# Maxima in pairs and a shared PSUM bank: a reordered attention step in a two-layer Fourier and attention kernel

## Chip, core and metric

The kernel runs on one core of one Trainium2 chip. Its time is device microseconds from the first to the last instruction of one execution; three runs are given, and beside them one execution was recorded by the hardware profiler. The engines that matter are PE (matmul), DVE (VectorE), ACT (ScalarE) and POOL (GpSimd). PE writes only to PSUM, which has eight banks of 512 fp32 values for each of 128 partitions; DVE and ACT read them from there.

## What is computed

The input is one sequence of 2048 tokens with 512 features. Two layers are run, and each adds two results to `x`: a Fourier mixing of the normalized `x`, and an attention with 32 heads of 16 values whose keys and values are shared by all heads.

```python
def _A_ref(x, dft_seq_re, dft_seq_im, dft_hid_re, dft_hid_im):
    a = jnp.einsum("bsd,ed->bse", x, dft_hid_re)
    b = jnp.einsum("bsd,ed->bse", x, dft_hid_im)
    return jnp.einsum("ts,bse->bte", dft_seq_re, a) - jnp.einsum("ts,bse->bte", dft_seq_im, b)

def _B_ref(x, wq, wk, wv, wo):
    ...
    scores = jnp.einsum("bhqd,bkd->bhqk", q, k) * (Dh ** -0.5)
    p = _softmax(scores, axis=-1)
    o = jnp.einsum("bhqk,bkd->bhqd", p, v)
    return o.transpose(0, 2, 1, 3).reshape(B, S, H * Dh) @ wo

x = x + _A_ref(_layernorm(x), ...)
x = x + _B_ref(_layernorm(x), wq, wk, wv, wo)
# the same two lines once more
```

All is fp32. The softmax subtracts each row's maximum, so the maximum of every row of 2048 scores must be known before the exponentials of that row.

## The kernel before

The order of the instructions is written out by hand: every engine runs its instructions in the order in which the Python code issues them, and waits for the others by semaphores. Each product of the mixing, of the projections and of the output is made of three reduced-precision products with the high and low parts of its operands (`mm3`, L86 to L89).

**Stages.** A layer has a mixing stage (`phase_a`) and an attention stage (`phase_b`). The mixing stage has 128 iterations `n`, each with four groups of three products into four accumulators (tile "x", two pairs of banks). After every 32 of them come four `y_tile`s, each a sum of 24 products into one bank, and then, among the next iterations, the transposes (`tr_tile`), the key and value projection (`kv`) and the query projection (`q_mm`) of these 512 tokens, each sum in one bank. Score maxima whose keys and queries are ready are found already here (`max_early`, listed in `EARLY` with the iterations over which they are spread: 16 entries of 32 units, 13 of them for later query tiles and kept in "mxe").

**A unit of maximum** is one product of 128 queries (all rows of one head of a pair) with 512 keys into a bank, and one DVE `reduce_max` of that bank to one column. A layer has 1520 such units left for the attention stage: the list `units`, in the order of query tile, head pair, key block, group.

**The attention stage** takes 16 query tiles `i` of 128 queries in 32 steps `s_` each, n = 32 i + s_. One step has:
- `pv`, the value product of the step two before: four products, side by side on the array, into the accumulator "z" (L712). After 16 steps ACT copies it to SBUF (L715).
- four scores (`score`, j = 0 to 3, L698): each 64 rows deep, so that the two groups g = 0 and 1 of heads use the two halves of the array's rows. Two scores share an "x" tile of two banks, and one exponential on ACT reads both banks (L701).
- maxima: `more_max` issues one unit (`max_half`, product at L347, reduction at L348), as many as `owed` allows, three a step. A unit is 64 rows deep as well and stands between the scores: score of group 1-g, one unit, score of group g, two units at most, score, score, one unit at most.
- tasks of the output: at step 12 of the next tile the output projection (`o_proj`): twelve products into a "y" bank, and after each half of them two more units; then the residual sum on DVE (L777). In layer 0 DVE also takes the statistics of the next normalization (steps 14 and 16).
- when a tile's maxima are all there, `max_neg` takes the last maximum on DVE and, two steps later, `max_rows` transposes it on PE into a "y" bank (L376) and ACT copies it out (L378); this happens at step 29 for the next tile, and at step 13 for the second half of tile 0.

**PSUM.** The eight banks are two "x" pairs (four banks), three "y" banks and one "z" bank. "y" serves single maxima, the sums of `y_tile`, `kv`, `q_mm` and the output projection, and the transpose of the maxima; "z" the transposes of the activations and the value accumulator. A tile's first product waits until all reads of the tile that had its bank before are done.

Of the kernel before, what the change touches and what calls it, by code (L numbers as in the profile page):

```python
# [8 lines left out]
F32 = mybir.dt.float32  # L9
F32R = mybir.dt.float32r  # L10
I32 = mybir.dt.int32
AF = mybir.ActivationFunctionType
# [5 lines left out]
P = 128  # L18
# [29 lines left out]
def fnet_mqa_kernel(ctx: ExitStack, tc: tile.TileContext, x_in, ct, dt_, wq, wkv, wo, out):  # L48
# [13 lines left out]
        return sb.tile([P, D], dtype, name=f"row{k}")  # L62

    def bank(tag):
        return ps.tile([P, 512], F32, name=tag, bufs={"y": 3, "z": 1}[tag])

    def pair():
        return ps.tile([P, 2, 512], F32, name="x", bufs=2)

    def split_ps(ps_, hi, lo, neg=False):  # L70
        nc.scalar.activation(hi, ps_, AF.Copy, scale=-1.0 if neg else 1.0)
# [115 lines left out]
    def make_layer(L, src, mid, dst, last):  # L187
# [66 lines left out]
                split_ps(v[0], xth, xtl)  # L254

        def kv(t0, n, xth, xtl, vt=None):
            pk = bank("y")[:, :n * P]
            for k in range(NK):
                mm3(pk, wkvh[:, k, :], wkvl[:, k, :], xth[:, k, :n * P], xtl[:, k, :n * P], k == 0, k == NK - 1)
            cs = slice(t0 * P, (t0 + n) * P)  # L260
            if vt is None:
                vt = half(7)[:64, :n * P]
            nc.scalar.copy(vt[32:64], pk[32:64])
            for g in range(2):
                gs = slice(64 * g, 64 * g + 64)
                nc.scalar.activation(kz[g][gs, cs], pk[gs], AF.Identity, scale=kmask[gs], bias=kone[gs])
            for g in range(2):
                gs = slice(64 * g + 32, 64 * g + 48)
                nc.vector.tensor_sub(kz[g][gs, cs], pk[gs], f(kz[g][gs, cs]))
            return vt  # L270
# [6 lines left out]

        def q_mm(tb, g, xth, xtl):
            wh, wl = st["wqh", g]
            pq = bank("y")  # L280
            for k in range(NK):
                ks = slice(k * P, (k + 1) * P)
                mm3(pq, wh[:, ks], wl[:, ks], xth[:, k, :], xtl[:, k, :], k == 0, k == NK - 1)
            hi = half(4 + 2 * (g % 2), F32R)
            lo = half(5 + 2 * (g % 2), F32R)
            split_act(pq, hi, lo, half(g))
            st["qs", tb, g] = hi, lo
# [41 lines left out]
                        nc.gpsimd.tensor_copy(o.mxp[i][:, :, :, kb], st["mxe"][:, e])  # L329
            return o.mxp[i]  # L330

        def max_one(i, pr, g, c0, n, to):
            pm = bank("y")[:, :n]
            nc.tensor.matmul(pm, o.qT[i][:, pr, :], kz[g][:, c0:c0 + n], start=True, stop=True)  # L334
            nc.vector.reduce_max(to, pm, axis=AX.X)  # L335

        def max_early(e, pr, g):
            i, kb = EARLY[e][:2]
            if "mxe" not in st:
                st["mxe"] = sb.tile([P, len(KEPT), NPAIR, 2], F32, name="mxe")  # L340
            to = st["mxe"][:, KEPT.index(EARLY[e]), pr, g:g + 1] if i else partial(0)[:, pr, g, kb:kb + 1]
            max_one(i, pr, g, kb * 512, 512, to)

        def max_half(i, pr, g, kb):
            pm = bank("y")
            gs = slice(64 * g, 64 * g + KR)
            nc.tensor.matmul(pm, o.qT[i][gs, pr, :], kz[g][gs, kb * 512:kb * 512 + 512], start=True, stop=True)  # L347
            nc.vector.reduce_max(partial(i)[:, pr, g, kb:kb + 1], pm, axis=AX.X)  # L348

        def qT_load(i, k=None):  # L350
            k_ = QSLOT[i] if k is None else k
# [19 lines left out]
            st["ms"] = ms  # L371

        def max_rows(i, p0=0, n=NPAIR, queue=None):
            queue = queue or nc.sync
            pt = bank("y")[:4 * n, :P]
            nc.tensor.transpose(pt, st["ms"].rearrange("p a b c -> p (a b c)"), ident)  # L376
            mt = sb.tile([64, P], F32R, name="mt")[:4 * n, :]
            nc.scalar.copy(mt, pt)  # L378
            for g in range(2):
                for r in range(2):  # L380
                    row = 64 * g + M0 + r
                    q = queue if r else nc.sync
                    q.dma_start(f(o.qT[i][row:row + 1, p0:p0 + n, :]), f(mt[n * (2 * g + r):n * (2 * g + r + 1), :]))

        def y_tile(tb, tt, zh, zl, x1, between={}):
            t = 4 * tb + tt
            y = bank("y")
            tsl = slice(tt * P, (tt + 1) * P)
            for cc in range(2):
                for k in range(NK):  # L390
                    mm3(y, zh[cc][:, k, tsl], zl[cc][:, k, tsl], dh[cc][:, k, :], dl[cc][:, k, :],
                        cc == 0 and k == 0, cc == 1 and k == NK - 1)
                    for fn in between.get(4 * cc + k, ()):
                        fn()
            nc.vector.tensor_add(x1, y, x1)
            nc.gpsimd.dma_start(mid[t], x1)
            ln_stats(x1, t)
# [103 lines left out]
        def phase_a(extra):  # L501
# [20 lines left out]
            for e, (i, kb, k, n0, n1, n2) in enumerate(EARLY):  # L522
                if n0 is not None:
                    add(n0, lambda i=i, k=k: qT_load(i, k))
                for u in range(2 * NPAIR):
                    at = divmod(int(4 * (n1 + u * (n2 - n1) / (2 * NPAIR))), 4)
                    b, n = divmod(at[0], 40)
                    at = (32 * b + n, at[1]) if n < 32 else ("y", b, 4 * (n - 32) + at[1])
                    inner.setdefault(at, []).append(lambda e=e, u=u: max_early(e, u // 2, u % 2))
            zh, zl, x1, vt = {}, {}, {}, {}  # L530
            z = None

# [121 lines left out]
                if g == 0:  # L654
                    v_tr(12, 4, vt[0])
            max_neg(0, 0, HALF, 5)
            for k in range(12):
                more_max()
                if k == 2:
                    max_rows(0, 0, HALF, nc.scalar)  # L660

        early = {e[:2] for e in EARLY}
        units = [(0, pr, g, 3) for pr in range(HALF, NPAIR) for g in range(2)]
        units += [(i, pr, g, kb) for i in range(1, NT) for pr in range(NPAIR) for kb in range(4) for g in range(2)
                  if (i, kb) not in early]
        o.done = o.extra = 0

        def more_max():
            if o.done < len(units) and units[o.done][0] in o.loaded | {0}:
                max_half(*units[o.done])  # L670
                o.done += 1

        def owed(n):
            return min(3 * (n + 1) + 12 + o.extra, len(units)) - o.done

        def done_with(i, pr):
            return all(u[:2] > (i, pr) for u in units[o.done:])

        ptiles = {}

        def score(i, s_, j):
# [4 lines left out]
                k = i * NSTEP + s_  # L686
                ptiles[i, s_] = slot((6, 7, 2)[k % 3]).rearrange("p (j n) -> p j n", j=4)
            w = j // 2
            if i == NT - 1 and jj == 1 and o.done == len(units):
                e = bank("y")  # L690
                nc.tensor.matmul(e, kz[g][64 * g:64 * g + KR, c * P:(c + 1) * P],
                                 o.qT[i][64 * g:64 * g + KR, cp:cp + 4, :], start=True, stop=True)
                nc.scalar.activation(ptiles[i, s_][:, j, :], e, AF.Exp, scale=DH ** -0.5)
                return
            first = "e" not in st
            if first:
                st["e"] = pair()
            nc.tensor.matmul(st["e"][:, g, :], kz[g][64 * g:64 * g + KR, c * P:(c + 1) * P],  # L698
                             o.qT[i][64 * g:64 * g + KR, cp:cp + 4, :], start=True, stop=True)
            if not first:  # L700
# [4 lines left out]
        def pv(i, s_):  # L705
# [6 lines left out]
                nc.tensor.matmul(a[32 * j:32 * j + 32, :], v1[:, c, :], pt[:, j, :], start=c == 0, stop=c == NT - 1)  # L712
            if c == NT - 1:
                oa = half(hf)
                nc.scalar.copy(oa, a)  # L715
                acc[i, hf] = oa

        bt = {}
# [48 lines left out]
        def o_proj(i):  # L767
            for k in range(NK):
                o_mm(k)
                if k % 2 and i < NT - 1:  # L770
                    for _ in range(2):
                        more_max()
                        o.extra += 1
            o_add(i)

        def o_add(i):
# [3 lines left out]
        def finish():  # L780
            i = NT - 1
            oa = acc.pop((i, 1))
            x_load(i)
            pt = bank("y")
            for b in range(4):
                nc.tensor.transpose(pt[:, b * P:(b + 1) * P], oa[:, b * P:(b + 1) * P], ident)
            o_mm(0)
# [5 lines left out]
            for jj in range(2):  # L793
# [1 line left out]
                    on[:, jj * P:(jj + 1) * P].rearrange("p (b g d) -> p b g d", b=4, g=2),  # L795
                    p4[:, :, 2 * jj:2 * jj + 2, :DH],
                    rc[:, :, 2 * jj:2 * jj + 2].unsqueeze(3).to_broadcast([P, 4, 2, DH]), op=ALU.mult)
            pt = bank("y")[:, :256]
            for jj in range(2):
                nc.tensor.transpose(pt[:, jj * P:(jj + 1) * P], on[:, jj * P:(jj + 1) * P], ident)  # L800
            split_ps(pt, bt["oh"][:, 256:], bt["ol"][:, 256:])
# [31 lines left out]
        def phase_b(nxt):  # L833
# [10 lines left out]
            for n in range(NT * NSTEP):  # L844
# [1 line left out]
                if len(behind) == 2:  # L846
                    pv(*behind.pop(0))
                behind.append((i, s_))
                g = units[o.done][2] if o.done < len(units) else 1
                for j, m in ((1 - g, 1), (g, 2), (3 - g, 0), (2 + g, 1)):  # L850
                    score(i, s_, j)
                    for _ in range(m):
                        if owed(n) >= 1:
                            more_max()
                if i == 0 and 2 <= s_ <= 8 and s_ % 2 == 0:
                    q_half_store(14, s_ // 2 - 1)
                if n == 12:
# [21 lines left out]
                nxt.a_start()  # L879
            for at in behind:  # L880
                pv(*at)
            return out_tasks(NT - 1)

        def half_tasks(i):
            return {
# [4 lines left out]
        def out_tasks(i):  # L890
            return {
                1: [lambda: o_store(i, 1), lambda: o_sum(i, 1), lambda: x_load(i)], 5: [lambda: o_inv(i, 1)],
                6: [lambda: o_load(i, 1)], 9: [lambda: o_scale(i, 1)], 10: [lambda: o_hi(i, 1)],
                12: [lambda: o_proj(i)], 14: [lambda: o_stats(i)], 16: [lambda: o_rstd(i)],
                25: [lambda: o_ln(i)], 26: [lambda: o_xnh(i)], 27: [lambda: o_xnl(i)],
            }

# [49 lines left out]
```

## Time and profile before

| | us |
|---|---|
| median of three runs (3771.49 to 3774.22) | 3773.21 |
| profiled execution, first to last instruction | 3768.5 |
| reductions of the attention stage's maxima (L348), DVE busy, 3040 of 684 ns | 1908.7 |
| exponentials of score pairs (L701), ACT busy, 1990 of 1027 ns | 1942.9 |
| value products (L712), PE busy, 8192 records | 1096.2 |
| scores into "x" (L698), PE busy, 2956 records in the largest group | 900.4 |
| maximum products of the attention stage (L347), PE busy, 2272 records in the largest group | 747.8 |
| early maxima (L335 into mxe), DVE busy, 832 | 525.2 |

The lines of the profile that carry the argument stand in the prediction. Busy times are the union of an instruction group's spans. A matmul's span is longer than what it keeps from the next one, since products overlap in the array; distances between starts tell more than durations. "Idle before" is the time in which an engine waited, with the line that ended the wait.

### The profile page before, as it was taken

What the parts mean: (1) busy time and instruction counts of PE and PEld (TensorE: products, weight loads), DVE (VectorE), ACT (ScalarE), POOL (GpSimd) and SP (SyncE); (2) the same over time, 40 slices, a digit from 0 to 9 for tenths busy, and PEclk for the clock granted to TensorE, in tenths of its full rate; (3) what the DMA queues carried; (4) which work ended last, traced back from release to release, by engine and by line L of the source; (5) the groups of instructions that cost most, each with busy time, mean ns of one, the idle gap of its engine ahead of it and who ended that gap; (6) DMA issues with size and microseconds to landing.
All of it is one profiled execution on the core that took longest, in us unless ns stands there. A gap on an engine that the chain in (4) does not pass through costs nothing.

```text
span 3768.5 us, 56828 instructions
## 1 busy us (share of the span) xinstructions
PE 3662.8 (97%) x21826; PEld 1982.0 (53%) x21826; DVE 2804.0 (74%) x4743; ACT 2371.4 (63%) x2846; POOL 831.8 (22%) x1009
## 2 busy tenths in 40 slices
PE   8989999999999999999999999999999999999999
PEld 6777778633433333333377777785334333333433
DVE  5165978688888888888411769777888888888882
ACT  3212211588888888888933221216888888888888
POOL 5634342211111111111155343421000000000000
PEclk9999999999999999999999999999999999999999
DMA  5543332311111100110133342413111111001100
GB/s 181 122 136 103 99 97 88 98 34 37 42 35 33 50 21 21 33 49 21 41 129 103 112 126 76 123 60 99 33 49 32 35 35 44 24 21 49 33 23 25
DMA packets 204704, 242.51 MB, mean 64 GB/s; under 512 B 36880, under 2 KB 160784, under 8 KB 197264
## 3 DMA queue, kind: packets, MB, share of 16 engines
q1 hardware_dynamic: 199504, 222.08, 19.6%
q0 software_dynamic: 4864, 16.78, 1.6%
q8 instruction: 171, 2.80, 0.3%
q14 instruction: 101, 0.83, 0.1%
q10 hardware_dynamic: 64, 0.02, 0.0%
HBM read 174.58 MB, written 63.17 MB: 63 GB/s over the span
## 4 chain that ended last, share of the span: by engine, by line
PE 82%; DVE 4%; ACT 3%; issue 3%; POOL 2%; DMA 1%; SPq 0%; POOLq 0%; ACTq 0%; DVEq 0%
PE z L712 25%; PE x L698 18%; PE y L347 11%; PE y L334 6%; PE x L87 5%; PE x L89 5%; PE x L88 5%; PE y L87 3%; DVE mxp L348 3%; PE y L89 2%; PE y L88 2%; ACT slot L701 1%; POOL row L182 1%; POOL cl L79 1%; POOL slot L84 1%
## 5 line engine op out<-in xcount | busy, mean ns | idle before, releaser
L701 ACT ACTIVATE slot<-x 128x1024 f32<-128x1024 f32 x1990 | 1942.9, 1027 | 334.8 <-PE x L698 267.1
L348 DVE TENSOR_REDUCE mxp<-y 128x1 f32<-128x512 f32 x3040 | 1908.7, 684 | 280.6 <-PE y L347 228.4
L712 PE MATMUL z<-slot,v 128*32 128x512 f32 x8192 | 1096.2, 605 | 1.9 <-ACT row L715 1.9
L698 PE MATMUL x<-slot,kz 64*128 64x512 f32 x2956 | 900.4, 446 | 4.4 <-DMA slot<-mt 3.8
L698 PEld LDWEIGHTS x<-slot,kz 64*128 64x128 f32 x2956 | 375.1, 185 | 732.1 <-ACT slot L701 597.9
L347 PE MATMUL y<-kz,slot 64*128 64x512 f32 x2272 | 747.8, 436 | 4.7 <-ACT mt L378 0.7
L335 DVE TENSOR_REDUCE mxe<-y 128x1 f32<-128x512 f32 x832 | 525.2, 684 | 122.7 <-PE y L334 121.7
L87 PE MATMUL x<-ch,xnh 128*128 128x512 f32 (+1 forms) x1152 | 432.6, 376 | 12.9 <-ACT xnh L449 8.5
L89 PE MATMUL x<-ch,xnl 128*128 128x512 f32 (+1 forms) x1152 | 429.7, 373 | 1.2 <-POOL xnl L450 0.7
L88 PE MATMUL x<-cl,xnh 128*128 128x512 f32 (+1 forms) x1152 | 427.9, 371 | 0.4 <-POOL cl L79 0.4
L334 PE MATMUL y<-kz,slot 128*128 128x512 f32 (+1 forms) x1088 | 380.4, 399 | 43.6 <-DMA slot<-qd 15.3
L752 POOL TENSOR_TENSOR row<-row,row 128x256 f32<-128x256 f32 x63 | 46.2, 734 | 1679.6 <-DMA row<-rd 971.3
L347 PEld LDWEIGHTS y<-kz,slot 64*128 64x128 f32 x2272 | 359.3, 185 | 99.0 <-DVE mxp L348 29.6
L78 ACT CAST ch<-craw 128x512 fp32r<-128x512 f32 x256 | 156.4, 619 | 387.9 <-PE x L89 366.0
L79 POOL TENSOR_TENSOR cl<-craw,ch 128x512 fp32r<-128x512 f32 x236 | 307.8, 1310 | 361.4 <-ACT ch L78 295.4
L712 PEld LDWEIGHTS z<-slot,v 128*32 128x32 f32 x8192 | 163.5, 108 | 276.7 <-issue 248.6
L334 PEld LDWEIGHTS y<-kz,slot 128*128 128x128 f32 x1088 | 203.3, 190 | 106.6 <-DVE mxe L335 27.4
L87 PEld LDWEIGHTS x<-ch,xnh 128*128 128x128 f32 x1152 | 219.5, 191 | 52.9 <-ACT xnh L449 8.5
L88 PEld LDWEIGHTS x<-cl,xnh 128*128 128x128 f32 x1152 | 219.3, 190 | 43.5 <-POOL cl L79 0.7
L89 PEld LDWEIGHTS x<-ch,xnl 128*128 128x128 f32 x1152 | 218.7, 190 | 44.6 <-POOL xnl L450 4.5
L335 DVE TENSOR_REDUCE mxp<-y 128x1 f32<-128x512 f32 (+1 forms) x256 | 146.0, 619 | 126.5 <-PE y L334 125.8
L87 PE MATMUL y<-slot,slot 128*128 128x512 f32 x384 | 156.6, 408 | 8.9 <-DVE mxp L348 5.8
(144 smaller groups left out, 2837.3 us busy)
## 6 DMA issues: line engine op xcount, KB each, us to landing
craw<-ct_in SPq DMA_DIRECT2D x112, 512.0 KB
slot<-qd SPq DMA_DIRECT2D x44, 1024.0 KB
qd<-row SPq DMA_DIRECT2D x144, 128.0 KB
od<-row SPq DMA_DIRECT2D x252, 64.0 KB
row<-x_in SPq DMA_DIRECT2D x32, 256.0 KB
mid<-row POOLq DMA_DIRECT2D x32, 256.0 KB, 2.3
craw<-ct_in SPq DMA_DIRECT2D x32, 256.0 KB
row<-mid SPq DMA_DIRECT2D x32, 256.0 KB
```

What stands on the lines that cost most here:

```text
L78: nc.scalar.copy(hi, raw)
L79: (eng or nc.vector).tensor_sub(lo, raw, f(hi))
L87: nc.tensor.matmul(ps_, ah, bh, start=start, stop=False)
L88: nc.tensor.matmul(ps_, ah, bl, start=False, stop=False)
L89: nc.tensor.matmul(ps_, al, bh, start=False, stop=stop)
L334: nc.tensor.matmul(pm, o.qT[i][:, pr, :], kz[g][:, c0:c0 + n], start=True, stop=True)
L335: nc.vector.reduce_max(to, pm, axis=AX.X)
L347: nc.tensor.matmul(pm, o.qT[i][gs, pr, :], kz[g][gs, kb * 512:kb * 512 + 512], start=True, stop=True)
L348: nc.vector.reduce_max(partial(i)[:, pr, g, kb:kb + 1], pm, axis=AX.X)
L698: nc.tensor.matmul(st["e"][:, g, :], kz[g][64 * g:64 * g + KR, c * P:(c + 1) * P], o.qT[i][64 * g:64 * g + KR, cp:cp + 4, :], start=True, ...
L701: nc.scalar.activation(ptiles[i, s_][:, 2 * w:2 * w + 2, :], st.pop("e"), AF.Exp, scale=DH ** -0.5)
L712: nc.tensor.matmul(a[32 * j:32 * j + 32, :], v1[:, c, :], pt[:, j, :], start=c == 0, stop=c == NT - 1)
```

## The change

The "y" tile has one bank instead of three, and a new tile "w" holds a pair of banks, one buffer of it. `long_bank` gives the sums of `y_tile`, `kv` and `q_mm` the banks "y" and "z" in turn. Early maxima take the two halves of "w" and then "y" (`one_bank(3)`), and in the `y_tile`s only the halves of "w" (`one_bank(2)`).

```diff
     def bank(tag):
-        return ps.tile([P, 512], F32, name=tag, bufs={"y": 3, "z": 1}[tag])
-
-    def pair():
-        return ps.tile([P, 2, 512], F32, name="x", bufs=2)
+        return ps.tile([P, 512], F32, name=tag)
+
+    def pair(tag="x"):
+        return ps.tile([P, 2, 512], F32, name=tag, bufs=2 if tag == "x" else 1)
+
+    turn = {"long": 0, "one": 0}
+
+    def long_bank():
+        turn["long"] += 1
+        return bank("yz"[turn["long"] % 2])
+
+    def one_bank(n):
+        k = turn["one"] % n
+        turn["one"] += 1
+        if k == 2:
+            turn["one"] = 0
+            return bank("y")
+        if k == 0:
+            turn["w"] = pair("w")
+        return turn["w"][:, k, :]
...
-            pk = bank("y")[:, :n * P]
+            pk = long_bank()[:, :n * P]
...
-            pq = bank("y")
+            pq = long_bank()
...
-        def max_one(i, pr, g, c0, n, to):
-            pm = bank("y")[:, :n]
+        def max_one(i, pr, g, c0, n, to, banks=2):
+            pm = one_bank(banks)[:, :n]
...
-            y = bank("y")
+            y = long_bank()
```

In the attention stage `more_max(2)` issues both groups of a head pair and key block into the two banks of "w", and one DVE instruction reduces both to two columns; `more_max(1)` issues one group into "y". The list of units now holds pairs, and the number owed per step is 25/8 with no extra units in the output projection. At the end of the mixing stage six pairs stand in the place of twelve single units.

```diff
-            for k in range(12):
-                more_max()
-                if k == 2:
+            for k in range(6):
+                more_max(2)
+                if k == 1:
                     max_rows(0, 0, HALF, nc.scalar)
...
+        def more_max(n):
+            if n == 2:
+                if o.next < len(units) and units[o.next][0] in o.loaded | {0}:
+                    i, pr, kb = units[o.next]
+                    turn["one"] = 0
+                    pm = pair("w")
+                    for g in range(2):
+                        max_mm(pm[:, g, :], i, pr, g, kb)
+                    nc.vector.reduce_max(partial(i)[:, pr, :, kb], pm, axis=AX.X)
+                    o.next += 1
+                    o.done += 2
+                return
...
+            i, pr, kb = o.odd
+            pm = bank("y")
+            max_mm(pm, i, pr, g, kb)
+            nc.vector.reduce_max(partial(i)[:, pr, g, kb:kb + 1], pm, axis=AX.X)
...
         def owed(n):
-            return min(3 * (n + 1) + 12 + o.extra, len(units)) - o.done
+            return min(25 * (n + 1) // 8 + 8, 2 * len(units)) - o.done
```

A step issues its first two scores, a pair of maxima, a single one, the last two scores (the group that the single unit didn't use comes first), and another single unit if one is still owed. The output projection goes ahead of the step's scores, right behind the value product, and the copy of the accumulator goes from ACT to DVE.

```diff
+                if i > 0 and s_ == 12:
+                    o_proj(i - 1)
+                g = 1 if o.odd else 0
+                score(i, s_, 0)
+                score(i, s_, 1)
+                if owed(n) >= 2:
+                    more_max(2)
+                if owed(n) >= 1:
+                    more_max(1)
+                score(i, s_, 3 - g)
+                score(i, s_, 2 + g)
+                if owed(n) >= 1:
+                    more_max(1)
...
             for k in range(NK):
                 o_mm(k)
-                if k % 2 and i < NT - 1:
-                    for _ in range(2):
-                        more_max()
-                        o.extra += 1
             o_add(i)
...
-                nc.scalar.copy(oa, a)
+                nc.vector.tensor_copy(oa, a)
```

Smaller parts: when all maxima are done, the second scores of every other step take "w" as a third pair (before, in the last tile, single "y" banks with an exponential each); the last transposes of the kernel use "w" and "z"; the transpose of the first maxima at the end of the mixing stage takes a `long_bank`.

More of the change, by code (lines that the diff above doesn't have):

```diff
@@ L330, in partial, with max_early @@
             return o.mxp[i]
-        def max_one(i, pr, g, c0, n, to):
-            pm = bank("y")[:, :n]
+        def max_one(i, pr, g, c0, n, to, banks=2):
+            pm = one_bank(banks)[:, :n]
             nc.tensor.matmul(pm, o.qT[i][:, pr, :], kz[g][:, c0:c0 + n], start=True, stop=True)
             nc.vector.reduce_max(to, pm, axis=AX.X)
-        def max_early(e, pr, g):
+        def max_early(e, pr, g, banks):
             i, kb = EARLY[e][:2]
@@ L341, in max_early, with max_mm @@
             to = st["mxe"][:, KEPT.index(EARLY[e]), pr, g:g + 1] if i else partial(0)[:, pr, g, kb:kb + 1]
-            max_one(i, pr, g, kb * 512, 512, to)
-        def max_half(i, pr, g, kb):
-            pm = bank("y")
+            max_one(i, pr, g, kb * 512, 512, to, banks)
+        def max_mm(pm, i, pr, g, kb):
             gs = slice(64 * g, 64 * g + KR)
             nc.tensor.matmul(pm, o.qT[i][gs, pr, :], kz[g][gs, kb * 512:kb * 512 + 512], start=True, stop=True)
-            nc.vector.reduce_max(partial(i)[:, pr, g, kb:kb + 1], pm, axis=AX.X)
         def qT_load(i, k=None):
@@ L373, in max_rows @@
         def max_rows(i, p0=0, n=NPAIR, queue=None):
+            pt = long_bank()[:4 * n, :P] if queue else bank("y")[:4 * n, :P]
+            nc.tensor.transpose(pt, st["ms"].rearrange("p a b c -> p (a b c)"), ident)
             queue = queue or nc.sync
-            pt = bank("y")[:4 * n, :P]
-            nc.tensor.transpose(pt, st["ms"].rearrange("p a b c -> p (a b c)"), ident)
             mt = sb.tile([64, P], F32R, name="mt")[:4 * n, :]
@@ L528, in phase_a @@
                     at = (32 * b + n, at[1]) if n < 32 else ("y", b, 4 * (n - 32) + at[1])
-                    inner.setdefault(at, []).append(lambda e=e, u=u: max_early(e, u // 2, u % 2))
+                    b = 3 if at[0] != "y" else 2
+                    inner.setdefault(at, []).append(lambda e=e, u=u, b=b: max_early(e, u // 2, u % 2, b))
             zh, zl, x1, vt = {}, {}, {}, {}
@@ L656, in phase_a @@
             max_neg(0, 0, HALF, 5)
-            for k in range(12):
-                more_max()
-                if k == 2:
+            for k in range(6):
+                more_max(2)
+                if k == 1:
                     max_rows(0, 0, HALF, nc.scalar)
         early = {e[:2] for e in EARLY}
-        units = [(0, pr, g, 3) for pr in range(HALF, NPAIR) for g in range(2)]
-        units += [(i, pr, g, kb) for i in range(1, NT) for pr in range(NPAIR) for kb in range(4) for g in range(2)
-                  if (i, kb) not in early]
@@ L666, in make_layer @@
[L666 to L671, printed above, removed]
+        units = [(0, pr, 3) for pr in range(HALF, NPAIR)]
+        units += [(i, pr, kb) for i in range(1, NT) for pr in range(NPAIR) for kb in range(4) if (i, kb) not in early]
+        o.next, o.done, o.odd = 0, 0, None
+        def more_max(n):
[10 more added lines that the diff above has]
+                return
+            if o.odd is None:
+                if o.next == len(units) or units[o.next][0] not in o.loaded | {0}:
+                    return
+                o.odd = units[o.next]
+                o.next += 1
+                g = 0
+            else:
+                g = 1
+            i, pr, kb = o.odd
+            pm = bank("y")
+            max_mm(pm, i, pr, g, kb)
+            nc.vector.reduce_max(partial(i)[:, pr, g, kb:kb + 1], pm, axis=AX.X)
+            o.done += 1
+            if g:
+                o.odd = None
@@ L673, in owed @@
         def owed(n):
-            return min(3 * (n + 1) + 12 + o.extra, len(units)) - o.done
+            return min(25 * (n + 1) // 8 + 8, 2 * len(units)) - o.done
         def done_with(i, pr):
-            return all(u[:2] > (i, pr) for u in units[o.done:])
+            return all(u[:2] > (i, pr) for u in units[o.next:] + ([o.odd] if o.odd else []))
         ptiles = {}
@@ L688, in score @@
             w = j // 2
[L689 to L694, printed above, removed]
             first = "e" not in st
             if first:
-                st["e"] = pair()
+                st["e"] = pair("w" if jj and s_ % 2 and o.done == 2 * len(units) else "x")
             nc.tensor.matmul(st["e"][:, g, :], kz[g][64 * g:64 * g + KR, c * P:(c + 1) * P],
@@ L783, in finish @@
             x_load(i)
-            pt = bank("y")
+            pt = pair("w")[:, 0, :]
             for b in range(4):
@@ L797, in finish @@
                     rc[:, :, 2 * jj:2 * jj + 2].unsqueeze(3).to_broadcast([P, 4, 2, DH]), op=ALU.mult)
-            pt = bank("y")[:, :256]
+            pt = bank("z")[:, :256]
             for jj in range(2):
@@ L848, in phase_b @@
                 behind.append((i, s_))
[L849 to L854, printed above, removed]
+                if i > 0 and s_ == 12:
[11 more added lines that the diff above has]
+                    more_max(1)
                 if i == 0 and 2 <= s_ <= 8 and s_ % 2 == 0:
@@ L881, in phase_b @@
                 pv(*at)
-            return out_tasks(NT - 1)
+            return {**out_tasks(NT - 1), 12: [lambda: o_proj(NT - 1)]}
         def half_tasks(i):
```

2 lines of the change are left out of this document (1 added, 1 removed).

## The prediction

> **What bounds the kernel now.** I read the page first (engine shares, chain of work), then the busy time by stage, then one attention step engine by engine.
>
> ```profile
> span 3768.5 us, 56828 instructions
> PE 3662.8 (97%) x21826; PEld 1982.0 (53%) x21826; DVE 2804.0 (74%) x4743; ACT 2371.4 (63%) x2846; POOL 831.8 (22%) x1009
> PE 82%; DVE 4%; ACT 3%; issue 3%; POOL 2%; DMA 1%; SPq 0%; POOLq 0%; ACTq 0%; DVEq 0%
> ...
> 0.00:715.80 715.80, 667.88 (x3063) 532.91 (x3063) 448.78 (x775) 182.28 (x332) 306.41 (x300) 0.98 0.40 115
> 715.80:1888.70 1172.90, 1162.10 (x7831) 456.85 (x7830) 980.45 (x1676) 1007.35 (x1102) 168.05 (x348) 1.00 0.13 37
> 1888.70:2588.70 700.00, 665.82 (x3090) 532.54 (x3086) 407.04 (x688) 173.94 (x310) 292.43 (x253) 0.99 0.34 105
> 2588.70:3757.20 1168.50, 1161.02 (x7828) 456.54 (x7827) 965.84 (x1601) 1005.92 (x1102) 64.89 (x108) 1.00 0.13 36
> ```
>
> The four lower rows are the stages (length, then busy time of PE, weight loads, DVE, ACT, POOL, then the granted clock): Fourier mixing and attention of layer 0, then of layer 1. Attention is 2341 of 3768 us; there PE is busy 99%, ACT 86%, DVE 83%, at full clock. One ordinary attention step, from the timeline of each engine:
>
> ```profile
> 1300.99 0.48 PE L698 MATMUL x<-xnh,kz 64*128 64x512 f32 x1
> 1300.99 0.71 PE L347 MATMUL y<-kz,slot 64*128 64x512 f32 x2
> 1301.33 0.39 PE L698 MATMUL x<-xnh,kz 64*128 64x512 f32 x1
> 1301.56 0.39 PE L347 MATMUL y<-kz,slot 64*128 64x512 f32 x1
> 1301.67 0.52 PE L698 MATMUL x<-xnh,kz 64*128 64x512 f32 x2
> 1302.11 1.06 PE L712 MATMUL z<-slot,v 128*32 128x512 f32 x8
> 1303.11 0.50 PE L698 MATMUL x<-xnh,kz 64*128 64x512 f32 x1
> ...
> 1301.82 1.94 ACT L701 ACTIVATE slot<-x 128x1024 f32<-128x1024 f32 x2 [0.20 <-PE x L698]
> ...
> 1301.55 1.89 DVE L348 TENSOR_REDUCE mxp<-y 128x1 f32<-128x512 f32 x3 [0.24 <-PE y L347]
> 1303.68 1.29 DVE L348 TENSOR_REDUCE mxp<-y 128x1 f32<-128x512 f32 x2 [0.24 <-PE y L347]
> ```
>
> I count time t in a step from the end of its value product (L712), here 1300.99. Scores and maximum products use half of the array's rows each, so two run together when they take different halves: seven of them make four rounds, beginning at t = 0.11 (after 0.11 of weight load), 0.34, 0.57 and 0.80; 0.32 after the last round begins the next value product starts (t = 1.12), and 1.00 later the next step (2.12). ACT idles 0.20 and DVE 0.24 per step, so PE sets it. A second look confirms that: here ACT had been idle 0.69, nothing of it could hold PE, and the value products still stand 2.11 apart.
>
> ```profile
> 1187.00 1.07 PE L712 MATMUL z<-slot,v 128*32 128x512 f32 x8
> 1188.82 1.94 ACT L701 ACTIVATE slot<-x 128x1024 f32<-128x1024 f32 x2 [0.69 <-PE y L347]
> 1189.11 1.07 PE L712 MATMUL z<-slot,v 128*32 128x512 f32 x8
> ```
>
> **The change part by part.** Seven or eight half-array products need four rounds in the old order and in the new one, so the reordering gives PE nothing in an ordinary step: 0. What it moves is who waits for a PSUM bank. Single maxima had three "y" banks; now they have one, shared with the output projection and the transpose of the maxima, and the pair has one "w" tile. PE issues in order, so whatever waits for "y" holds the scores and the value product behind it, and ACT after them.
>
> *When is "y" free?* Three rows price the reductions, two show a waiting PE:
>
> ```profile
> L348 DVE TENSOR_REDUCE mxp<-y 128x1 f32<-128x512 f32 x3040 | 1908.7, 684 | 280.6 <-PE y L347 228.4 <-PE x L698 47.0
> L335 DVE TENSOR_REDUCE mxp<-y 128x1 f32<-128x256 f32 x64 | 24.8, 421 | 13.3 <-PE y L334 12.9
> L701 ACT ACTIVATE slot<-x 128x1024 f32<-128x1024 f32 x1990 | 1942.9, 1027 | 334.8 <-PE x L698 267.1 <-PE y L347 63.2 <-PE y L691 1.3
> ...
> 1191.18 3.65 DVE L348 TENSOR_REDUCE mxp<-y 128x1 f32<-128x512 f32 x6
> 1193.09 0.18 PEld L347 LDWEIGHTS y<-kz,xnl 64*128 64x128 f32 x1 [0.42 <-DVE mxp L348]
> 1193.76 1.07 PE L712 MATMUL z<-slot,v 128*32 128x512 f32 x8
> ```
>
> From 256 to 512 elements a reduction grows by 263 ns, so 1024 would take 684 + 526 = 1.21 us. Six in a row take 3.65, one each 0.594, so a follower starts 0.09 before the end: the pair holds DVE for 1.12. No row has a two-bank reduction on DVE: below it stands ACT's 1.027 for the same shape, above it two whole singles, 1.37; I take 1.21, which lies on DVE's own line, and prices beyond are rivals. A reduction starts 0.45 after its product's round (1300.99 + 0.11 to 1301.55). The pair's halves sit in round two: start 0.79. The single follows on DVE at 1.91 and ends at 2.59; the load waiting for a bank follows a reduction's end by 0.04 (third of the six ends at 1191.18 + 2 x 0.594 + 0.684 = 1193.05, load at 1193.09). So "y" is free at **t = 2.63**.
>
> *The fourth unit.* The owed count is 25(n+1)//8 + 8: three units a step, four where n%8 = 7. With 1520 units per layer it lasts to n = 483, so 60 such steps per layer, 120 in all. There the second single is issued last and waits for "y" of the first: 2.63 instead of round four. Its product begins 0.11 later, the value product 0.32 after that: 3.06 against 1.12, **1.94 each, +233 us**. Nothing covers it: DVE must first reduce the pair, and PE's next work is queued behind.
>
> By the Trainium skill, Perfetto Trace Analysis, section Matmuls, independent matmul groups should rotate through PSUM banks so that one is read out while the next is computed; it speaks against giving the singles one bank, and the 0.42 wait in the row above (three banks, six reductions late) agrees.
>
> *The transpose of the maxima* (two steps after each maximum is closed) goes into "y" too, right after the scores.
>
> ```profile
> 1220.25 0.49 PE L698 MATMUL x<-slot,kz 64*128 64x512 f32 x1
> ...
> 1221.60 0.30 PE L376 MATMUL y<-ident,ms 128*64 128x128 f32 x1
> 1221.83 1.07 PE L712 MATMUL z<-slot,v 128*32 128x512 f32 x8
> ```
>
> It starts at t = 1.35 now and would start at 2.63: +1.28, 16 times a layer (15 at step 29, one at step 13 of the first tile): **+41 us**.
>
> *The output projection* moves ahead of the scores and loses its four maxima.
>
> ```profile
> 1400.48 1.07 PE L712 MATMUL z<-slot,v 128*32 128x512 f32 x8
> 1402.86 0.19 PEld L87 LDWEIGHTS y<-slot,slot 128*128 128x128 f32 x1 [0.51 <-issue]
> 1403.19 0.39 PE L88 MATMUL y<-slot,slot 128*128 128x512 f32 x1
> 1403.42 0.40 PE L89 MATMUL y<-slot,slot 128*128 128x512 f32 x1
> ...
> 1406.91 1.07 PE L712 MATMUL z<-slot,v 128*32 128x512 f32 x8
> 1408.22 0.68 DVE L777 TENSOR_TENSOR row<-y,row 128x512 f32<-128x512 f32 x1
> ...
> 1409.61 0.16 PEld L712 LDWEIGHTS z<-slot,v 128*32 128x32 f32 x8 [0.36 <-issue]
> ```
>
> Now the step takes 6.43 and the next 2.70: 4.89 over two ordinary ones. After: it waits for "y" until 2.63 - 2.12 = 0.51; twelve products at 0.234 (1403.42 - 1403.19) and some 0.2 for the two changes of array shape make 3.01; the next single then waits for the residual add: last product begins at 3.20, add at 3.65, done 4.33, load 4.37 against 3.52 + 0.46 = 3.98, 0.39. In all 3.91: 0.98 less, 15 tiles, two layers: **-29 us**.
>
> *Ordinary steps.* The single's weights would load at 2.12 + 0.46 = 2.58, "y" is free at 2.63. Half of the steps wait 0.05 (a step made late gives the next one slack): 0.025 on some 800: **+20 us**.
>
> *Copies of the accumulator* go from ACT to DVE.
>
> ```profile
> L715 ACT COPY row<-z 128x512 f32<-128x512 f32 x64 | 38.0, 594 | 1.3 <-PE z L712 1.1
> ```
>
> On ACT the copy delays exponentials for which PE waits; on DVE it delays the pair, and "y", by about 0.2 (DVE is done with the step before at t = 0.4, then copies 0.6; the pair was due at 0.79). Between 13 us less and 13 more over 64 copies; I take 0. In layer 0 the normalization statistics on DVE do the same: +6. At the end of each mixing stage six pairs take the place of twelve singles: five waits of 0.04 + 0.56 + 1.21 = 1.81 against nine reductions of 0.594: **+3.7 a layer, +7**.
>
> *Mixing stages.* Early maxima take w, w, y in turn, and in the y sums w, w alone.
>
> ```profile
> L335 DVE TENSOR_REDUCE mxe<-y 128x1 f32<-128x512 f32 x832 | 525.2, 684 | 122.7 <-PE y L334 121.7
> PEld y L334 <- DVE mxe L335: 27.4, 60, 2.3
> ```
>
> A new pair must wait for both halves of the old one. In the y sums that drains DVE: about 54 of 512 units a layer, 27 pairs, up to 0.60 (0.04 + 0.56) each: 16 us. Elsewhere the "y" reduction (0.594) covers the drain but for some 0.1 on 150 rounds: 15. Nothing if the wait goes by halves; I take 20 of 0 to 35 a layer, **+40**.
>
> Sum: 233 + 41 - 29 + 20 + 6 + 7 + 40 = +318. The profiled execution has 3768.5 of span and the runs a median of 3773.2, 4.7 around it, which stays: 3773 + 318 = **4091 us**, 8.4% slower.
>
> **Rivals.**
> - *The pair is read faster.* If DVE needed only 0.60 for 1024 elements, "y" would be free at 2.11: 1.42 x 120 = 170, 0.76 x 32 = 24, no wait in ordinary steps, other terms kept: 170 + 24 - 29 + 13 + 40 gives 3991. For it: no row shows the form. Against: three lengths of one engine lie on a line with 1 ns an element. 9%.
> - *The pair is read slower*, a fixed cost per bank: 1.37 for the pair, 1.28 of it ahead of the follower, "y" at 2.79. Fourth units 252, transposes 46, ordinary steps 0.105 x 800 = 84, others as before: about 4180. 9%.
> - *Faster: ACT becomes the bound.* Both first scores now stand in round one, so the first exponential starts 0.23 earlier and ACT's 0.20 gap closes. If PE could keep up, steps would fall from 2.12 to ACT's 1.94: 0.18 x 960 = 173, and 29 from the projection: 3571. It decides only if four rounds and a value product fit 1.94, and if the fourth unit's wait is under 0.2 us (29 us over 120 steps). Against: the 2.11 step with a rested ACT. 5%.
> - *One read for two tiles.* The pair spares DVE 2 x 0.594 - 1.12 = 0.07 on some 980 pairs, 66 us. It counts only where DVE ends the wait; in ordinary steps DVE idles 0.24. If it counted and "y" did not hold PE: 3773 - 66 - 29 = 3678. 3%. [...]
>
> **How the numbers follow.** My forecast has 74%, its own range 4040 to 4140 (0 to 35 a layer in mixing, 0.1 us either way on the fourth unit). The faster-read case and the slower-read case lie on either side; 3985 to 4165 takes in the first and half of the second, leaving out the two fast rivals (8%) and some 9% of the rest. Slower by over 0.2% (about what a measurement of this kernel can tell from no change): 74 + 9 + 9 = 92%; faster: 7%; no change: 1%.
>
> **What would show it.** Intervals between value products in the profile after: about 2.12 to 2.17 in ordinary steps, some 4.06 at steps 7, 15, 23, 31, with the weight load of the maximum waiting about 1.8 for DVE; the transpose likewise; the two steps at the projection 0.98 shorter together; PE's busy share in attention down to about 90%; a pair reduction near 1.21. If steps 7, 15, 23 and 31 are no longer than their neighbours, the forecast is wrong; if steps stand at 1.94, ACT's rival is right.

## The result, and the profile after

The kernel after takes 4452.8 us (median of four runs, 4444.2 to 4474.8) against 3773.7 before: a ratio of 1.181, 95% interval 1.178 to 1.184. The prediction said 4091, with 3985 to 4165 as its range. The direction came true, and so did the waits that it named in the attention stage; the size didn't: +679 us instead of +318.

The stages of the kernel after (length, busy time of PE, weight loads, DVE, ACT and POOL, granted clock, DMA share, GB/s), in the same order as before:

```profile
0.00:877.90 877.90, 734.49 (x3059) 527.80 (x3059) 466.68 (x765) 182.34 (x332) 305.65 (x300) 0.96 0.32 95
877.90:2228.10 1350.20, 1224.66 (x7833) 448.31 (x7831) 976.56 (x1228) 996.59 (x1043) 168.02 (x348) 0.96 0.11 32
2228.10:3099.90 871.80, 743.50 (x3085) 536.98 (x3084) 425.94 (x679) 173.46 (x308) 291.24 (x253) 0.95 0.27 85
3099.90:4440.60 1340.70, 1224.32 (x7833) 449.58 (x7831) 960.63 (x1153) 996.79 (x1043) 64.80 (x108) 0.96 0.11 31
```

Attention grew from 1172.9 and 1168.5 to 1350.2 and 1340.7, together 349.5 us; the mixing stages, in which only the first two of a layer's 512 attention steps fall, from 715.8 and 700.0 to 877.9 and 871.8, together 333.9. The granted clock, 1.00 in attention before, is 0.96. The sum, 683, is the whole difference of the two spans (4452.0 and 3768.5).

A step with four units in the attention stage after (PE, weight loads, DVE; the batch-norm rows between them are left out):

```profile
1000.22 0.50 PE L729 MATMUL x<-slot,kz 64*128 64x512 f32 x2
...
1000.56 0.40 PE L362 MATMUL w<-kz,slot 64*128 64x512 f32 x2
...
1000.79 0.39 PE L362 MATMUL y<-kz,slot 64*128 64x512 f32 x1
1000.79 0.62 PE L729 MATMUL x<-slot,kz 64*128 64x512 f32 x2
...
1001.36 1.20 DVE L690 TENSOR_REDUCE mxp<-w 128x2 f32<-128x1024 f32 x1
1002.47 0.68 DVE L705 TENSOR_REDUCE mxp<-y 128x1 f32<-128x512 f32 x1
1003.20 0.18 PEld L362 LDWEIGHTS y<-kz,slot 64*128 64x128 f32 x1 [2.22 <-DVE mxp L705]
1003.21 0.49 PE L362 MATMUL y<-kz,slot 64*128 64x512 f32 x1 [1.79 <-DVE mxp L705]
1003.62 0.16 PEld L743 LDWEIGHTS z<-slot,v 128*32 128x32 f32 x8 [0.24 <-issue]
1003.63 1.81 PE L743 MATMUL z<-slot,v 128*32 128x512 f32 x8
...
1005.37 0.80 PE L729 MATMUL x<-slot,kz 64*128 64x512 f32 x2
```

The order is the forecast one: two scores, the pair, the single, two scores, all issued within 0.8 us; then nothing on PE until DVE has reduced the pair (L690) and the single (L705) and the fourth unit's weights load at 1003.20, 0.05 after the single's reduction ends. The value product behind it, which took 1.00 before its successor could start, now takes 1.74 (1003.63 to 1005.37). A view by stretches of the same place tells why:

```profile
1000.00:1003.80 3.80, 2.01 (x16) 0.94 (x16) 3.18 (x7) 2.51 (x3) 0.00 (x0) 1.00 0.00 0
1003.80:1007.20 3.40, 3.40 (x15) 1.17 (x7) 1.19 (x2) 0.94 (x1) 0.00 (x0) 0.50 0.02 5
1007.20:1011.00 3.80, 3.66 (x27) 1.31 (x27) 3.71 (x8) 3.05 (x4) 1.44 (x8) 1.00 0.10 21
```

For 3.4 us after the stall PE was granted half its clock (0.50). The two-bank reduction itself came out as estimated, 1225 ns against 1.21 us:

```profile
L690 DVE TENSOR_REDUCE mxp<-w 128x2 f32<-128x1024 f32 x978 | 1198.2, 1225 | 489.2 <-PE w L362 479.8
...
L705 DVE TENSOR_REDUCE mxp<-y 128x1 f32<-128x512 f32 x1084 | 739.4, 682 | 72.0 <-PE y L362 72.0
...
L350 PE MATMUL w<-kz,slot 128*128 128x512 f32 x720 | 352.5, 490 | 192.2 <-DVE mxe L351 133.1 <-DVE mxp L351 33.4 <-DMA slot<-qd 15.7
```

Adding up the distances between value products of both layers, while maxima are issued (964 steps), by the kind of step:

| steps | before, us | after, us | difference | predicted |
|---|---|---|---|---|
| 120 with n%8 = 7 (four units after) | 255.7 | 494.8 | +239 | +233 |
| 120 that follow them | 265.2 | 326.9 | +62 | 0 |
| 30 with the transpose (step 29) | 77.2 | 116.3 | +39 | +41 (32 of them) |
| 28 pairs of steps 12 and 13 around the projection (6.40 + 2.70 and 6.05 + 2.12 each) | 254.8 | 228.6 | -26 | -27 (-29 for 30) |
| all other steps of these 964 | 1371.9 | 1411.7 | +40 | +26 |
| the last steps of the layers, without maxima | | | -4 | 0 |
| mixing stages | 1415.8 | 1749.7 | +334 | +47 |

So the terms for the waits of the attention stage hold to within some 14 us each, and two things are missing from the sum: 62 us and more of low clock, and 287 us in the mixing stages. There PE waits for reductions of early maxima ahead of w products for 133.1 + 33.4 us in the last row above, and it is granted half its clock for 154 us instead of 50.

In the mixing stage after, a stretch with many early maxima looks like this (PE, weight loads and DVE; the products of the mixing between them are left out):

```profile
496.30 0.19 PEld L350 LDWEIGHTS w<-kz,slot 128*128 128x128 f32 x1 [0.53 <-DVE mxe L351]
...
496.41 0.19 PEld L350 LDWEIGHTS y<-kz,slot 128*128 128x128 f32 x1
...
496.84 0.69 DVE L351 TENSOR_REDUCE mxe<-w 128x1 f32<-128x512 f32 x1 [0.59 <-PE w L350]
...
497.58 0.19 PEld L350 LDWEIGHTS w<-kz,slot 128*128 128x128 f32 x1 [0.30 <-DVE mxe L351]
...
498.12 0.69 DVE L351 TENSOR_REDUCE mxe<-w 128x1 f32<-128x512 f32 x1
...
498.86 0.19 PEld L350 LDWEIGHTS w<-kz,slot 128*128 128x128 f32 x1 [0.53 <-DVE mxe L351]
499.20 0.39 PE L350 MATMUL y<-kz,slot 128*128 128x512 f32 x1
```

The turn is w, y, w, w, y. Every w product, the second half of a pair included (the one at 498.86 is a second half), loads its weights only when the reduction of the w half before it has ended, here 0.05 us later. Over both stages none of the 784 w loads comes earlier than that after the w reduction before it, and 621 come within 0.1 us of its end. The prediction had let the second half run beside the first.

### The profile page after: what moved, and what is told of

It is laid out like the page before. It is cut to its first block, busy times and chain, and to the rows that moved or that the text cites. A ratio compares the mean times of both kernels' runs of the same rounds, so it can differ in the third digit from the quotient of the medians.

```text
span 4452.0 us, 55770 instructions
## 1 busy us (share of the span) xinstructions
PE 3932.9 (88%) x21826; PEld 1965.7 (44%) x21826; DVE 2832.4 (64%) x3829; ACT 2350.4 (53%) x2724; POOL 829.7 (19%) x1009
## 5 line engine op out<-in xcount | busy, mean ns | idle before, releaser
L732 ACT ACTIVATE slot<-x 128x1024 f32<-128x1024 f32 x2018 | 1964.8, 1024 | 692.6 <-PE x L729 685.5
L690 DVE TENSOR_REDUCE mxp<-w 128x2 f32<-128x1024 f32 x978 | 1198.2, 1225 | 489.2 <-PE w L362 479.8
L743 PE MATMUL z<-slot,v 128*32 128x512 f32 x8192 | 1148.2, 629 | 3.7 <-DVE row L746 3.2
L705 DVE TENSOR_REDUCE mxp<-y 128x1 f32<-128x512 f32 x1084 | 739.4, 682 | 72.0 <-PE y L362 72.0
L351 DVE TENSOR_REDUCE mxe<-w 128x1 f32<-128x512 f32 x590 | 406.6, 689 | 259.2 <-PE w L350 259.2
L350 PE MATMUL w<-kz,slot 128*128 128x512 f32 (+1 forms) x784 | 380.9, 486 | 207.1 <-DVE mxe L351 133.1
L362 PE MATMUL y<-kz,slot 64*128 64x512 f32 x808 | 361.0, 447 | 135.9 <-DVE mxp L705 132.8
L350 PEld LDWEIGHTS w<-kz,slot 128*128 128x128 f32 x784 | 153.5, 196 | 420.0 <-DVE mxe L351 305.5
L362 PE MATMUL w<-kz,slot 64*128 64x512 f32 x1464 | 302.6, 410 | 12.8 <-DVE mxp L690 11.5
L362 PEld LDWEIGHTS y<-kz,slot 64*128 64x128 f32 x808 | 154.3, 191 | 301.4 <-DVE mxp L705 282.5
```

Source lines behind the costliest of these rows:

```text
L690: nc.vector.reduce_max(partial(i)[:, pr, :, kb], pm, axis=AX.X)
L732: nc.scalar.activation(ptiles[i, s_][:, 2 * w:2 * w + 2, :], st.pop("e"), AF.Exp, scale=DH ** -0.5)
```

## The experiments

The kernel before was timed again beside each (3772.7 to 3773.7 us). Ratios are to it. "Step" figures are means over the tiles of the distance between value products.

**Three banks again, new order kept.** The first question was whether the banks make the whole loss.

```diff
-        return ps.tile([P, 512], F32, name=tag)
+        return ps.tile([P, 512], F32, name=tag, bufs={"y": 3, "z": 1}[tag])
...
-        return bank("yz"[turn["long"] % 2])
+        return bank("y")
...
-                    pm = pair("w")
-                    for g in range(2):
-                        max_mm(pm[:, g, :], i, pr, g, kb)
-                    nc.vector.reduce_max(partial(i)[:, pr, :, kb], pm, axis=AX.X)
+                    for g in range(2):
+                        pm = bank("y")
+                        max_mm(pm, i, pr, g, kb)
+                        nc.vector.reduce_max(partial(i)[:, pr, g, kb:kb + 1], pm, axis=AX.X)
...
```

(`one_bank` gives "y" as well, and where w served as a third pair or in the kernel's last transposes, "x" and "y" stand in its place.)

> The new order of the step, the owed count, the projection ahead of the scores and the copy on DVE stay; the banks go back to three single y banks, every maximum is a single reduction, long sums use y. Theory A (the waits for y and w make all of the loss): no step at 7, 15, 23, 31 over 2.3 us, both mixing stages back at 700 to 720 us, the projection's step near 5.3, in all 3700 to 3750 us. Rival B (the new order itself, the copy on DVE or the fourth unit on PE costs): above 3800 us, with steps over 2.2 us in the attention stage.

Measured: 3879.5 us, 1.0285 (1.0268 to 1.0302). Mixing is back at 717.1 and 701.2, so the banks make that loss, and no half-speed stretch begins in attention. But attention still takes 1231.0 and 1217.2: steps 7, 15, 23 and 31 take 2.97 (2.93 in layer 1), ordinary ones 2.12 and 2.24 in turn. Theory A was wrong to give all of the loss to the banks; the order and the fourth unit cost something with three banks too.

**Own tiles for the two halves, in the mixing stages alone.**

```diff
...
-        if k == 0:
-            turn["w"] = pair("w")
-        return turn["w"][:, k, :]
+        return bank("uv"[k])
...
+            stage(f"att{L}")
             for k in range(6):
                 more_max(2)
```

(`stage` closes one set of PSUM tiles and opens the next: u, v and y for mixing, w and y for attention.)

> As after, but in the mixing stages the two halves of w are two tiles of their own, one bank each; same order of banks, attention unchanged. Theory A (the two halves of one tile wait for each other's reduction, so a w product loads only after the last w reduction): mixing stages fall from 878 and 872 us to 715 to 760 each, in all 4120 to 4200 us. Rival B (the turn w, w, y, the long sums in y and z, or the clock hold PE): mixing stays above 820 each, in all above 4350 us.

Measured: 4131.9 us, 1.0953 (1.0928 to 1.0979).

```profile
0.00:726.50 726.50, 663.15 (x3059) 529.99 (x3059) 446.04 (x765) 182.37 (x332) 305.96 (x300) 0.98 0.38 114
726.50:2076.90 1350.40, 1224.21 (x7833) 448.54 (x7831) 976.23 (x1228) 996.39 (x1043) 167.36 (x348) 0.96 0.11 32
2076.90:2788.40 711.50, 664.02 (x3083) 531.87 (x3082) 405.10 (x679) 173.49 (x308) 291.70 (x253) 0.98 0.33 104
2788.40:4126.80 1338.40, 1222.18 (x7835) 449.13 (x7835) 959.97 (x1153) 996.61 (x1043) 64.64 (x108) 0.96 0.11 31
```

Mixing falls to 726.5 and 711.5, 312 us less, with the same banks in the same turn; attention stays. The clock of the mixing stages recovers with it, from 0.96 and 0.95 to 0.98. What is left of the loss there is 22 us, against 47 in the prediction's sum (40 for the early maxima, 7 for the six pairs at the end).

**One half only.** This tells whether the two halves of a pair wait for each other, or only a new pair for the old one.

```diff
-        if k == 0:
-            turn["w"] = pair("w")
-        return turn["w"][:, k, :]
+        turn["w"] = pair("w")
+        return turn["w"][:, 0, :]
```

> As after, but every early maximum outside y takes the first half of a fresh w pair, never the second. Theory A (the two halves of one tile already wait for each other): nothing changes, 4430 to 4475 us, mixing stages at 870 to 885. Rival (a new pair waits for both halves of the old one, while the second half runs beside the first): every second half gains a wait of 0.5 us or more, 780 of them: 4600 us or more.

Measured: 4444.6 us, 1.1779 (1.1755 to 1.1803); mixing 885.3 and 866.6. A second bank that is half of the same tile is worth nothing: the halves wait for each other. Together with the run before, the wait follows the tile, not the bank: the program's PSUM pools keep their waits by tile (`reuse_waits="tile"`).

**The first single ahead of the pair, in steps of four.**

```diff
-                if owed(n) >= 2:
+                if owed(n) >= 4:
+                    more_max(1)
                     more_max(2)
-                if owed(n) >= 1:
-                    more_max(1)
+                else:
+                    if owed(n) >= 2:
+                        more_max(2)
+                    if owed(n) >= 1:
+                        more_max(1)
```

> As after, but in a step of four units the first single goes ahead of the pair, so that DVE reduces it first and y is free 1.1 us earlier. Theory A (the fourth unit waits for DVE to get through pair and single): steps 7, 15, 23, 31 fall from 4.08 to about 2.95 us, 134 us less. On the clock: if the half-speed stretches in the following steps come from PE sitting idle about 1.9 us, they become rarer with 0.8 us idle and up to 84 us more go: 4230 to 4320 us. Rival B (something else ends the wait): steps stay at 4.0 us, 4440 us.

Measured: 4266.5 us, 1.1310 (1.1288 to 1.1333). The attention stages after this edit:

```profile
874.90:2135.00 1260.10, 1201.92 (x7833) 440.38 (x7831) 969.90 (x1228) 994.52 (x1043) 167.54 (x348) 0.99 0.12 34
...
3003.80:4248.70 1244.90, 1195.09 (x7833) 438.17 (x7831) 953.25 (x1153) 994.16 (x1043) 64.73 (x108) 1.00 0.11 34
```

Steps of four fall from 4.12 to 3.19 (forecast 2.95), 112 us. The steps behind them, on which nothing was edited, fall from 2.72 to 2.12, 73 us, and the granted clock returns to 0.99 and 1.00: of the 57 half-speed stretches that began in the attention stages 6 are left, all behind the transpose of step 29. DVE's queue before the fourth unit is what PE waits for, and the long stall is what lowers the clock in the steps behind it.

**The fourth unit behind the next value product.**

```diff
                 behind.append((i, s_))
+                if n and owed(n - 1) >= 1:
+                    more_max(1)
...
                 score(i, s_, 2 + g)
-                if owed(n) >= 1:
-                    more_max(1)
```

> As after, but the fourth unit is issued behind the next step's value product. Theory A (PE issues in order, so only the place matters; y is free 0.5 us into the next step): step 7 falls to 2.15 us, step 8 rises to about 3.4 at full clock since its own single then waits for the fourth unit's reduction; the two together 5.5 instead of 6.2, and fewer half-speed stretches: 4290 to 4380 us. Rival B (DVE's work for the fourth unit is what costs): the two steps together stay at 6.2 us or more, 4430 us or more.

Measured: 4287.3 us, 1.1365 (1.1342 to 1.1388), a little below the range. Steps of four take 2.14, the next 3.48: the two together 5.62 where the kernel after takes 6.85 and the kernel before 4.34. The same unit in the same bank, reduced by the same engine, costs 1.2 us less; half of this is clock, since the step behind a fourth unit takes 2.72 in the kernel after and 2.12 where the clock stays up (the run above). 4 half-speed stretches are left in attention. PE takes its matmuls in the program's order, so what stands behind the waiting instruction has a part in the price.

**Both repairs.** Own tiles in mixing and the single ahead of the pair.

> As after, with both edits: own tiles for the early maxima's two banks and the first single ahead of the pair in steps of four. If the two costs are separate (halves of w in the mixing stages; DVE's order before the fourth unit in the attention stages), the gains add: 4453 - 321 - 186 = 3946, 3925 to 3970 us, mixing stages at 715 to 730 and attention at 1245 to 1260. If they share a cause (a clock that stays low from one stage to the next), less than the sum: above 4000 us.

Measured: 3951.7 us, 1.0475 (1.0456 to 1.0493), with stages of about 726, 1254, 712 and 1246 us. The two gains, 321 and 186, add up to within 6 us, so the two costs are separate. What remains over the kernel before, 178 us, lies in the steps of four (128), the transposes (39), the ordinary steps (33) and the mixing stages (22); shorter steps around the projection (27) and some smaller gains come off.

**The order alone.** Back at the kernel before, with the scores' order as the one edit.

```diff
-                for j, m in ((1 - g, 1), (g, 2), (3 - g, 0), (2 + g, 1)):
+                for j, m in ((0, 0), (1, 3), (3 - g, 0), (2 + g, 1)):
```

> Before, with one edit: the first two scores come ahead of all three maxima of a step. The prediction priced this order at nothing. Theory C (maxima start a round later, so the third reduction ends 0.23 us later and the next step's third unit waits for its bank): ordinary steps alternate 2.12 and 2.24 us as in the run with three banks, some 900 steps by 0.06: 3815 to 3840 us. Rival (the order is free): 3765 to 3785 us.

Measured: 3820.5 us, 1.0122 (1.0105 to 1.0139). Two steps of that run (PE, the reductions of the first step, and weight loads):

```profile
1301.10 0.50 PE L698 MATMUL x<-slot,kz 64*128 64x512 f32 x2
...
1302.23 1.07 PE L712 MATMUL z<-slot,v 128*32 128x512 f32 x8
1303.22 0.49 PE L698 MATMUL x<-slot,kz 64*128 64x512 f32 x2
...
1304.47 1.06 PE L712 MATMUL z<-slot,v 128*32 128x512 f32 x8
...
1301.87 1.89 DVE L348 TENSOR_REDUCE mxp<-y 128x1 f32<-128x512 f32 x3 [0.37 <-PE y L347]
...
1301.55 0.18 PEld L347 LDWEIGHTS y<-kz,slot 64*128 64x128 f32 x1 [0.15 <-DVE mxp L348]
...
1303.81 0.18 PEld L347 LDWEIGHTS y<-kz,slot 64*128 64x128 f32 x1 [0.28 <-DVE mxp L348]
```

The third maximum loads at 0.45 and at 0.59 after its step's scores. With the scores first, the maxima start a round later. DVE ends its third reduction 2.66 after the step's first scores (1301.87 + 1.89 - 1301.10), where in the step of the prediction it was 2.45 (1301.55 + 1.89 - 1300.99), and the next step's third unit finds its bank still taken in every second step: 0.11 there, 47 us in all. The reordering isn't free.

**The old order, the projection moved.** An attempt at a kernel faster than both: the projection ahead of the scores without its four units, these as a fourth unit behind the value product of every eighth step, three banks.

```diff
-            return min(3 * (n + 1) + 12 + o.extra, len(units)) - o.done
+            return min(25 * (n + 1) // 8 + 12, len(units)) - o.done
...
-                if k % 2 and i < NT - 1:
-                    for _ in range(2):
-                        more_max()
-                        o.extra += 1
...
+                if n and owed(n - 1) >= 1:
+                    more_max()
+                if i > 0 and s_ == 12:
+                    o_proj(i - 1)
...
-                        if owed(n) >= 1:
+                        if q and owed(n) >= 1:
+                            q -= 1
                             more_max()
...
```

(`q` starts each step at 3, so that the scores have three units at most among them.)

> Before, with the output projection ahead of the scores and without its four units; these come as a fourth unit every eighth step, behind the next step's value product. Three y banks, old order of scores, copy on ACT. Theory (a bank is free there, so the unit costs PE 0 to 0.25 us, and the projection's two steps shorten by about 1.5): 3735 to 3765 us. Rival (a fourth unit costs a bank wait of 0.6 to 0.8 us wherever it stands): 3800 us or more.

Measured: 3812.6 us, 1.0102 (1.0087 to 1.0117): a miss. The projection's step falls to 5.49 and the one behind it to 2.12, 1.5 us less for the two, but steps with a fourth unit take 2.96. The fourth unit itself finds a bank; now the third unit of the same step waits for one (0.71 at 2697.45, for instance). The waits of all maxima for banks, in this run and then in the kernel before:

```profile
PEld y L347 <- DVE mxp L348: 202.3, 302, 0.8
...
PEld y L347 <- DVE mxp L348: 38.3, 118, 0.5
```

Four units close together in three banks cost 0.8 us at both places of the fourth that were run (2.97 and 2.96 for the step that holds them); spread over the projection, as before, four cost 1.5 together.

**The copy on DVE alone.**

```diff
-                nc.scalar.copy(oa, a)
+                nc.vector.tensor_copy(oa, a)
```

> Before, with one edit: the 64 copies of the accumulator go from ACT to DVE. Prediction: between 13 us less and 13 us more, 3760 to 3787 us. Rival (the copy puts maxima so late that PE waits at each of them for more than 0.3 us): above 3792 us.

Measured: 3779.0 us, 1.0013 (1.0004 to 1.0022). Some 5 us for 64 copies, inside the bounds of the prediction.

## Why the prediction was right and wrong

- **PE sets the step, four rounds and a value product, 2.12:** right. Ordinary steps after take 2.12 and 2.18 in turn, as the wait of 0.05 in half of the steps asked for. The whole group came to +40 against +26 (20 for these waits, 6 for the statistics): in layer 0 the step behind the statistics (step 17) takes 2.70 instead of 2.12, some 8 us by itself.
- **The price of a pair's reduction (1.21 us) and the moment "y" is free (2.63):** right, 1.225 measured; the fourth unit's load at 1003.20 stands 2.98 after the step's scores, because the normalization statistics of layer 0 came ahead of the pair in that step (14 of the 120), but the median of the 120 is 2.65, and on average a step of four takes 4.12 against 4.06. With 1.225 both rivals on the speed of this reduction (0.60 and 1.37) fall.
- **The fourth unit, +233:** measured +239; the edits that moved it or changed DVE's order took about half of the cost away (112 us, and 1.3 us left of 2.5), in the direction that the mechanism says. **The transpose, +41,** measured +39 for the 30 at step 29; **the projection, -29,** measured 0.93 a pair of steps against 0.98; **the copy, 0,** measured +5 alone; **the six pairs, +3.7 a layer,** measured +4.2 from the last reduction ahead of them to the first value product (15.8 us against 11.6).
- **"The reordering gives PE nothing in an ordinary step: 0"** was right for PE's rounds and left out that the maxima start a round later. Alone it costs 47 us. In the kernel after, the same delay was inside the moment at which "y" is free, so the sum did not suffer.
- **The step that failed: "A new pair must wait for both halves of the old one. [...] Elsewhere the "y" reduction (0.594) covers the drain but for some 0.1 on 150 rounds: 15."** It took the two halves of one w tile for two independent banks. They wait for each other, so each w unit costs a full turn of product, reduction and wait (497.58 to 498.86: 1.28 us) in place of 0.594. The term was sized at 40, with 70 as its end; own tiles gave back 312 us, and half a tile was as good as a whole one. These 312 us hold what the waits did to the clock of the mixing stages as well.
- **The term that was missing: the clock.** The prediction read "at full clock" off the kernel before and kept it. The stalls lowered it: the steps behind a fourth unit lose 62 us, and half-speed stretches take 207 us of the attention stages and 154 of the mixing stages (5 and 50 in the kernel before, where none begins in attention). The Trainium skill, TensorE: Matmul & The Clock Gate, Part 1 on the clock gate, says that the clock falls to half after about 3.4 us without work on PE. The half-speed stretches here last 3.41 us or a multiple of it, which fits its window; but the gaps that set them off in attention are shorter here: 1.79 us in the rows above, 1.38 to 1.47 in 106 of the 120 steps of four.
- **Rivals.** None of the fast ones held: no step was shorter than 2.10 while maxima ran, so none came near ACT's 1.94, and no gain from DVE's saving per pair shows in the table. The range was too narrow since no rival stood for a wait between halves or for a lower clock. That the direction held is no luck: the waits of the attention stage alone, as forecast, made the kernel slower.

The kernel before stays the fastest of all that were run.

## What to carry to other kernels

Before a PSUM bank is shared or paired, write down for each waiting instruction when its bank comes free and what stands behind it on PE: the same unit cost 2.5 us over two steps ahead of a value product, lower clock included, and 1.3 us behind it. Two banks in one tile are one buffer when the waits are kept per tile, so give independent results tiles of their own. And a repeated PE stall can be paid twice, as here with gaps of 1.4 us and more: once as the stall and again as a lower clock behind it.

## What was not expected of the hardware

In the kernel after, PE stands idle for 1.38 to 1.47 us in 106 of the 120 steps of four, and for 1.78 to 1.81 us in the 14 in which the statistics come first. All 57 half-speed stretches that began in attention began behind these gaps; behind the 30 gaps of 1.2 to 1.3 us at step 29 none did. With the single ahead of the pair, the gaps in steps of four are 0.31 to 0.44 us and no stretch begins behind them; the 6 that are left begin behind step 29.

The traces also show what decides which of the equal gaps is punished. In each of them the starts of all half-speed stretches lie on one raster of 3.413 us, to within 0.01 us. Of the 120 gaps, 75 lay whole in one interval of the raster, and in 55 cases the next interval was at half speed; 45 were cut by the border of two intervals, and behind only 2 of these was it so. The stall at 1001.41 to 1003.20 above lies whole in the interval that ends at 1003.8. So PE's idle time inside one interval counts, not the length of the gap alone. A sharp limit is not shown: of the 68 whole gaps of 1.38 to 1.47 us, 48 were followed by half speed and 20 were not, and of the 24 whole gaps at step 29 none was in the kernel after, but 6 were with the single ahead of the pair.
